# Low parts of the last expert's activations: VectorE alone instead of VectorE and GpSimd

## The chip, the cores and the metric

The kernel runs on one core of a Trainium2 chip. The metric is the device time of one execution in microseconds (us), lower is better. Engines are called as the profile calls them: PE is TensorE (PEld its weight loads), DVE is VectorE, ACT is ScalarE, POOL is GpSimd, SP is SyncE, which here only issues transfers.

## What is computed

Attention with a sliding window and four sink positions, then two mixtures of eight experts, all in float32. The first mixture gives every token to every expert and weighs the results; the second gives each token to exactly one expert, 192 tokens each, chosen greedily in the order of the gate's logits. Cut to what matters here:

```python
def _moe_ref(x, w_gate, w1, w2):          # N, D, E, F = 1536, 512, 8, 1024
    P = ...                               # gate weights, balanced over 8 rounds
    for e in range(E):
        h = np.maximum(x @ w1[e], 0.0)
        out += P[:, e:e + 1] * (h @ w2[e])

def _moe2_ref(x, w_gate, w1, w2):
    logits = x @ w_gate
    ...                                   # sort, assign each token, cap = N // E
    for e in range(E):
        mask = assigned == e
        out[mask] = np.maximum(x[mask] @ w1[e], 0.0) @ w2[e]
```

## The kernel before

A float32 product is made of three passes of a faster format: each operand is split into a high part (rounded) and a low part (what is left), and high x high, high x low and low x high are added up. For an activation tile h of 128 x 256 the high part `hh` is a copy by ACT and the low part `hl` a subtraction, h - hh.

The first mixture runs expert by expert over six groups of 256 tokens and eight chunks of 128 hidden units. Its last expert (number 7, `LE`) is done differently. Its first product (L1148, `make_pair_g1`) is finished early and its activations are kept as float32 for all groups (tiles `h7`, `xp0`, `xp1`; `h32_of`). From them `make_last_pair` makes the last expert's share of the second mixture's logits with two small matmuls for each tile (L1519, L1521), and so the logits are known before the last expert's second product is. That product is *deferred* (`make_deferred`): for each of 6 groups x 8 chunks = 48 tiles it splits h again (`make_parts`) and issues six matmuls (L1083, in `make_g2`), two for each of the three passes. So `make_parts` is called 96 times, 48 for the logits and 48 for the deferred product. Its low part is line 1553, its high part line 1550. The tiles `hh` and `hl` go round in a ring of four.

The deferred product is what PE does during the *routing* (`make_routing`), which finds for every expert the threshold of its logits. It is a chain of eight rounds. In a round DVE masks and reduces (L1675 to L1683, L1694), DVE writes eight and ACT four comparison tiles (L1688, L1691), PE counts with twelve small matmuls (L1698), DVE closes the round (L1701 to L1704), and PE broadcasts the result (L1708), for which the next L1675 waits. Then tokens are ranked, positions written (L1792), and a flag says if the simple routing holds (L1767). POOL scatters the tokens' rows into sorted order in DRAM (L1892). After the flag every engine passes a branch (L1801), whose body is not executed for these inputs. The second mixture begins with the load of the sorted rows (L1934); their memory is handed over once all deferred parts have been made. Then come the transposes (L2002, L2009) and the second mixture's products (L2043 and on).

The order of all this is not written by hand. A greedy list scheduler (`Sched`) runs when the program is built: each task has an engine or a choice of engines, a cost in us, a priority and dependences; the scheduler keeps a clock for each engine, takes the task that can start first (within a small slack the most urgent), and writes its instructions. Where a task has a choice, the engine on which it would end first gets it:

```python
k = (t + (cost if len(x.alts) > 1 else 0.0), pr)
```

Where PE's clock shows a hole ahead of its next task, `Sched.warm` writes dummy transposes of the identity (L206) into it, one for each 0.11 us of the modelled hole. These instructions stand in the program and are executed whatever the real hole is. So a change of one task's engines moves the order of everything behind it. `PLO` is the cost that the scheduler has for a low part on POOL, 0.88; on DVE it is 0.43.

Of the kernel before, what the change touches and what calls it, by code (L numbers as in the profile page):

```python
# [22 lines left out]
def tile_attention_moe_moe(ctx, tc, q, k, v, n_sink, window, wg1, w1a, w2a, wg2, w1b, w2b, out):  # L23
# [26 lines left out]
    def f32(ap):  # L50
        return ap.bitcast(F32)
# [33 lines left out]
    class Sched:  # L85
# [11 lines left out]
        def task(self, eng, cost, fn, deps=(), prio=0.0, use=(), acq=None, rel=None, name=""):  # L97
            x = Task()
            x.name = name
            x.alts = [(eng, cost)] if isinstance(eng, str) else list(zip(eng, cost))  # L100
            x.fn, x.prio, x.acq, x.rel, x.succ, x.end, x.eng = fn, prio, acq, rel, [], None, None
            d = set(deps)
            for h in use:
                assert not h.closed
                if not h.users:
                    if h.prev is not None:
                        assert h.prev.users
                        d.update(h.prev.users)
                        h.prev.closed = True
                    if h.last is not None:  # L110
                        d.add(h.last.users[0])
                h.users.append(x)
            d.discard(None)
            x.deps = list(d)
            x.left = 0
            for y in x.deps:
                if y.end is None:
                    y.succ.append(x)
                    x.left += 1
            if not x.left:  # L120
                self.ready.append(x)
            return x
# [119 lines left out]
    PLO, PSP = 0.88, 1.35  # L242
# [177 lines left out]
    task = sch.task  # L420
# [1071 lines left out]
    def h32_of(g, c):  # L1492
        if g not in H7:
            p = g // 2
            x = xp.tile([P, 2, FC, GW], F32, name=f"xp{p - 1}") if p else raws["pool"].tile([P, 2, FC, GW], F32, name="h7", bufs=1)
            H7[2 * p], H7[2 * p + 1] = x[:, 0], x[:, 1]
        return H7[g][:, c]

    def make_last_pair(k):
# [5 lines left out]
        for i in range(2):  # L1505
            g, s = 2 * p + i, ("p", k, i)
            hh_ = ring["h"].new()

            def relu(g=g, i=i):
                act(h32_of(g, fc), HS[k, 0][:, i], AF.Relu)  # L1510

            H32[g, fc] = task("ACT", 0.39, relu, deps=[prev, G1E.get(p - 1)] + [H32.get((g - i, fc))], prio=pr - 33.0 + i, use=[hph],
                              name="relu")
            a, b = make_parts(s, g, fc, hh_, pr - 29 + i)

            def gmm(i=i, s=s):
                o = bank[key][:, i * GW:(i + 1) * GW]
                hh, hl = HT[s]
                nc.tensor.matmul(o[:2 * E], W2G[:, fc].rearrange("p s e -> p (s e)"), hh, start=first and i == 0, stop=False,  # L1519
                                 skip_group_check=True)  # L1520
                nc.tensor.matmul(o[:E], W2G[:, fc, 0], hl, start=False, stop=last and i == 1, skip_group_check=True)  # L1521

            m = task("PE", 0.22, gmm, deps=[a, b, GDEP[1], LAST.get("gmm")], prio=pr - 5, use=[hh_],
                     acq=key if first and i == 0 else None, name="gmm")
            LAST["gmm"] = m
# [21 lines left out]
    def make_parts(s, g, fc, hh_, pr):  # L1547
        def hi():
            HT[s] = (wk.tile([P, GW], F32R, name="hh", bufs=4), wk.tile([P, GW], F32R, name="hl", bufs=4))
            act(HT[s][0], h32_of(g, fc), AF.Copy)  # L1550

        def lo(eng):
            (nc.gpsimd if eng == "POOL" else nc.vector).tensor_tensor(HT[s][1], h32_of(g, fc), f32(HT[s][0]), op=OP.subtract)  # L1553

        a = task("ACT", 0.41, hi, deps=[H32[g, fc]], prio=pr, use=[hh_], name="hhi")
        return a, task(("DVE", "POOL"), (0.43, PLO), lo, deps=[a], prio=pr, use=[hh_], name="hlo")

    DEF = []

    def make_deferred(q_):  # L1560

        n = n_moe1 + q_ // 2
        g = q_ // (2 * NU)
        _, _, u = uses[n]
        f = q_ % 2
        fc = 2 * u + f
        s = ("d", q_)
        k = q_ % (2 * NU)
        make_loads_for(n)
        pr = v_gem(v_use(n) + f)  # L1570
        hh_ = ring["h"].new()
        a, b = make_parts(s, g, fc, hh_, pr - 32.5)
        DEF.extend((a, b))
        make_g2(s, hh_, [a, b], pr + 5.0, (LE, g, n, f, k == 0, k == 2 * NU - 1), dyn=True)
# [676 lines left out]
```

## Time and profile before

| what | us |
|---|---|
| median of 3 runs | 1373.38 |
| lowest, highest | 1371.47, 1374.92 |
| the profiled execution's time | 1374.58 |
| its span in the profile | 1372.8 |

The profiled execution is one more execution, with its own time; the span runs from its first to its last recorded instruction. Busy times are sums over instructions of an engine. The windows view gives them for stretches of the span, with the clock that PE was granted (1.00 is 2.4 GHz, its higher level; 0.5 is 1.2 GHz, the lower one) and the mean busy share of the 16 DMA engines. The timeline view gives instructions one by one; in brackets stands the idle time just before one and what ended it. Matmuls are pipelined, so the distance from one start to the next is what one costs.

### The profile page before, as it was taken

The numbers are of one execution on the slowest core, as the hardware profiler recorded it, in microseconds if no ns is written. First come the engines' busy times: TensorE is split into PE (matmuls) and PEld (weight loads), VectorE is DVE, ScalarE is ACT, GpSimd is POOL, SyncE is SP. The second block draws the span as 40 slices with busy tenths as digits, with TensorE's granted clock in tenths as the row PEclk, the third lists the DMA queues.
The fourth block names the chain that finished last, engine by engine and source line by source line (L and its number), as shares of the span: only waits on it lengthen the run. The fifth ranks groups of instructions, "written<-read, shape, count | busy, mean of one in ns | idle before, by whom it ended". The sixth has DMA issues, their size and how long they took to land. (4 is left out here: it accounts for less than half of the span.)

```text
span 1372.8 us, 22527 instructions
## 1 busy us (share of the span) xinstructions
PE 1355.2 (99%) x8299; PEld 1173.3 (85%) x8299; DVE 928.3 (68%) x2455; ACT 620.3 (45%) x1560; POOL 112.3 (8%) x251
## 2 busy tenths in 40 slices
PE   8999999999999999999999999999999999899998
PEld 8888888988888888888998889888887777688887
DVE  8877767886455555646364645449989968568885
ACT  7777663644243333334242433331133353357874
POOL 4221110000000000000000000000001023401111
PEclk9999999999999999999999999999999999989999
DMA  7433211112020101001010101161020010458873
GB/s 172 131 78 78 63 39 47 62 47 78 0 62 16 46 17 47 31 32 47 16 62 1 63 1 62 47 202 40 16 93 16 1 47 17 131 199 263 263 225 98
DMA packets 102529, 101.47 MB, mean 74 GB/s; under 512 B 42248, under 2 KB 79112, under 8 KB 102288
## 3 DMA queue, kind: packets, MB, share of 16 engines
q1 hardware_dynamic: 100432, 93.71, 22.5%
q0 software_dynamic: 1984, 6.30, 1.5%
q8 instruction: 66, 1.08, 0.3%
q14 instruction: 47, 0.39, 0.1%
HBM read 91.71 MB, written 8.28 MB: 73 GB/s over the span
## 5 line engine op out<-in xcount | busy, mean ns | idle before, releaser
L1347 ACT ACTIVATE hh<-c 128x256 fp32r<-128x256 f32 x180 | 74.6, 415 | 124.8 <-DVE c L1314 112.2
L1148 PE MATMUL hp<-xp,w1hs 128*128 128x512 f32 x384 | 120.8, 396 | 0.0
L1314 DVE TENSOR_TENSOR c<-hp,cp 128x256 f32<-128x256 f32 x120 | 50.8, 423 | 94.7 <-PE hp L1290 89.5
L1378 PE MATMUL o<-w2ls,hh 128*128 128x512 f32 x240 | 95.0, 396 | 0.0
L1378 PE MATMUL o<-w2hs,hh 128*128 128x512 f32 x240 | 94.4, 393 | 0.0
L1378 PE MATMUL o<-w2hs,hl 128*128 128x512 f32 x240 | 94.3, 393 | 0.0
L1290 PE MATMUL hp<-xp,w1hs 128*128 128x256 f32 x480 | 88.1, 282 | 0.0
L1148 PEld LDWEIGHTS hp<-xp,w1hs 128*128 128x128 f32 x384 | 69.5, 188 | 15.1
L1350 DVE SCALAR_TENSOR_TENSOR hl<-c,hh 128x256 fp32r<-128x256 f32 x180 | 74.5, 419 | 9.4 <-ACT hh L1347 7.1
L1290 PEld LDWEIGHTS hp<-xp,w1hs 128*128 128x128 f32 x480 | 76.6, 188 | 4.7
L1553 POOL TENSOR_TENSOR hl<-h,hh 128x256 fp32r<-128x256 f32 x15 | 12.9, 857 | 789.7 <-ACT hh L1550 786.0
L1148 PE MATMUL hp<-xp,w1ls 128*128 128x512 f32 x192 | 75.8, 395 | 0.0
L1052 PE MATMUL hp<-xp,w1hs 128*128 128x256 f32 x384 | 73.9, 287 | 0.5 <-DVE xp L708 0.3
L1306 ACT ACTIVATE cu<-hp 128x256 f32<-128x256 f32 x60 | 23.1, 385 | 108.0 <-PE hp L1290 107.9
L1083 PE MATMUL o<-w2hs,hh 128*128 128x512 f32 x168 | 68.4, 407 | 1.6 <-PEq L1801 1.6
L1290 PE MATMUL hp<-xp,w1ls 128*128 128x256 f32 x240 | 67.5, 281 | 0.0
L1347 ACT ACTIVATE hh<-hp 128x256 fp32r<-128x256 f32 x60 | 23.2, 386 | 96.6 <-PE hp L1290 96.4
L882 DVE TENSOR_TENSOR w2ls<-w2r,w2hs 128x512 fp32r<-128x512 f32 x89 | 59.7, 684 | 10.4 <-DVEq L1801 6.1
L1083 PE MATMUL o<-w2ls,hh 128*128 128x512 f32 x168 | 66.5, 396 | 0.0
L1083 PE MATMUL o<-w2hs,hl 128*128 128x512 f32 x168 | 66.4, 395 | 0.0
L884 ACT ACTIVATE w2hs<-w2r 128x512 fp32r<-128x512 f32 x92 | 56.5, 624 | 18.5 <-DMA w2r<-in_moe_w_dram 11.6
L882 DVE TENSOR_TENSOR w1ls<-w1r,w1hs 128x512 fp32r<-128x512 f32 x85 | 57.9, 687 | 9.2 <-ACT w1hs L884 8.6
(484 smaller groups left out, 4028.3 us busy)
## 6 DMA issues: line engine op xcount, KB each, us to landing
w1r<-in_moe_w_dram SPq DMA_DIRECT2D x46, 512.0 KB, 4.3
w2r<-in_moe_w_dram SPq DMA_DIRECT2D x46, 512.0 KB, 3.6
wr<-in_moe_w_dram SPq DMA_DIRECT2D x46, 512.0 KB, 3.4
xs<-xs_d SPq DMA_DIRECT2D x14, 256.5 KB, 4.1
nk<-in_k_dram SPq DMA_DIRECT2D x12, 256.0 KB, 3.1
nq<-in_q_dram SPq DMA_DIRECT2D x12, 256.0 KB, 3.9
nv<-in_v_dram SPq DMA_DIRECT2D x12, 256.0 KB, 3.6
wgb<-wgd SPq DMA_DIRECT2D x1, 2048.0 KB
```

Source lines behind the costliest of these rows:

```text
L882: (nc.gpsimd if eng == "POOL" else nc.vector).tensor_tensor(lo[:, c], r[:, c], f32(hi[:, c]), op=OP.subtract)
L884: act(hi[:, c], r[:, c], AF.Copy)
L1052: nc.tensor.matmul(p, a, b, start=(c == 0 and j == 0), stop=(c == DC - 1 and j == 2), skip_group_check=True)
L1083: nc.tensor.matmul(OUTP[g, j], a_, b_, start=(first and i == 0), stop=(last and i == 2), skip_group_check=True)
L1148: nc.tensor.matmul(HS[k, 0].rearrange("p a b -> p (a b)"), a, b, start=(c == 0 and j == 0), stop=(c == DC - 1 and j == 2), skip_group_chec ...
L1290: nc.tensor.matmul(st[bk], l_[:, c], r_[:, c], start=(start and c == 0 and j == 0), stop=(c == 1 and j == 2), skip_group_check=True)
L1306: act(st[key], st[bk], AF.Copy)
L1314: tt(st[out], st[bk], st[key], op=OP.add)
L1347: act(hh, st[key], AF.Relu)
L1350: nc.vector.scalar_tensor_tensor(HT[i, f, t][1], st[key], 0.0, f32(HT[i, f, t][0]), op0=OP.max, op1=OP.subtract)
L1378: nc.tensor.matmul(OUTP[g, j % GT], a_, b_, start=(first and f == 0 and z == 0), stop=(last and f == 1 and z == 2), skip_group_check=True)
L1553: (nc.gpsimd if eng == "POOL" else nc.vector).tensor_tensor(HT[s][1], h32_of(g, fc), f32(HT[s][0]), op=OP.subtract)
```

## The change

A low part of `make_parts` could be made by DVE or POOL, whichever the scheduler's clocks showed to end it first. It is now a task of DVE alone, with the cost that DVE had.

```diff
@@ make_parts @@
         a = task("ACT", 0.41, hi, deps=[H32[g, fc]], prio=pr, use=[hh_], name="hhi")
-        return a, task(("DVE", "POOL"), (0.43, PLO), lo, deps=[a], prio=pr, use=[hh_], name="hlo")
+        return a, task("DVE", 0.43, lambda: lo("DVE"), deps=[a], prio=pr, use=[hh_], name="hlo")
```

The line also reorders the program from the last expert on. Counted over the whole order, POOL has 35 instructions of line 1553 before and none now, DVE 61 and 96, and PE has 225 dummy transposes of line 206 before and 356 now; all other counts are equal.

On POOL, around the constants of the routing (`rpiv`) and the first scatters. `h` and `xp` are the tiles that hold the activations, `acc` a group's output rows. Before:

```order
L1615 IOTA rpiv 128x128
L1553 TENSOR_TENSOR hl<-h_11287,hh 128x256 x11
L1553 TENSOR_TENSOR hl<-xp_11547,hh 128x256 x12
L1553 TENSOR_TENSOR hl<-xp_11807,hh 128x256 x3
L1891 MEMSET spacer 1x1
L1892 DMA xs_d<-acc_111,pos 3072x513
```

And now:

```order
L1615 IOTA rpiv 128x128
L1891 MEMSET spacer 1x1
L1892 DMA xs_d<-acc_111,pos 3072x513
L1891 MEMSET spacer 1x1
L1892 DMA xs_d<-acc_112,pos 3072x513
```

The 26 subtractions between the constants and the first scatter are gone from POOL (eight stood ahead of the constants, one among the scatters).

On DVE, from the comparison tiles of one routing round to the start of the next. Before:

```order
L1694 TENSOR_SCALAR rOHh<-rOHb 128x32
L1688 TENSOR_SCALAR rG<-rT,ru 128x128 x8
L1553 TENSOR_TENSOR hl<-xp_11547,hh 128x256
L1701 TENSOR_SCALAR rinc<-side_12605 8x1
L1702 SCALAR_TENSOR_TENSOR rjk,rinc<-side_12605,rinc,rdT 8x128
L1704 SCALAR_TENSOR_TENSOR rinc<-rinc 8x1
L1099 SCALAR_TENSOR_TENSOR acc_113<-side_12445,PR,acc_113 128x512
L1675 TENSOR_TENSOR rV<-rVh,o_12643 128x96
```

And now:

```order
L1694 TENSOR_SCALAR rOHh<-rOHb 128x32
L1688 TENSOR_SCALAR rG<-rT,ru 128x128 x8
L1553 TENSOR_TENSOR hl<-h_11287,hh 128x256
L1701 TENSOR_SCALAR rinc<-o_12460 8x1
L1702 SCALAR_TENSOR_TENSOR rjk,rinc<-o_12460,rinc,rdT 8x128
L1704 SCALAR_TENSOR_TENSOR rinc<-rinc 8x1
L1553 TENSOR_TENSOR hl<-h_11287,hh 128x256
L1675 TENSOR_TENSOR rV<-rVh,side_12496 128x96
```

Before, DVE had 8 low parts between the routing's first reduction (L1645) and the flag (L1767), in some rounds none; now it has 18, two in most rounds.

On PE, from one round's broadcast (L1708) on. `side`, `o` and `av` are PSUM banks, `w2hs` and `w2ls` the parts of the weights. Before, eighteen to twenty deferred matmuls stand between one broadcast and the next:

```order
L1708 MATMUL side_12296<-ident,rinc 128x8
L1083 MATMUL side_12281<-w2hs_121,hh 128x512
L1083 MATMUL av<-w2ls_122,hh 128x512
L1083 MATMUL side_12281<-w2ls_122,hh 128x512
L1083 MATMUL av<-w2hs_121,hl 128x512
L1083 MATMUL side_12281<-w2hs_121,hl 128x512
L1083 MATMUL av<-w2hs_10250,hh 128x512
L1083 MATMUL side_12281<-w2hs_10250,hh 128x512
L1083 MATMUL av<-w2ls_10251,hh 128x512
L1083 MATMUL side_12281<-w2ls_10251,hh 128x512
L1083 MATMUL av<-w2hs_10250,hl 128x512
L1083 MATMUL side_12281<-w2hs_10250,hl 128x512
```

And now, up to the round's first count:

```order
L1708 MATMUL o_12428<-ident,rinc 128x8
L1083 MATMUL av<-w2hs_10250,hl 128x512
L1083 MATMUL side_12277<-w2hs_10250,hl 128x512
L1083 MATMUL av<-w2hs_10250,hh 128x512
L1083 MATMUL side_12277<-w2hs_10250,hh 128x512
L1083 MATMUL av<-w2ls_10251,hh 128x512
L1083 MATMUL side_12277<-w2ls_10251,hh 128x512
L1083 MATMUL av<-w2hs_10250,hl 128x512
L1083 MATMUL side_12277<-w2hs_10250,hl 128x512
L206 MATMUL side_12452<-ident 128x128 x7
L1698 LDWEIGHTS rOHb
```

Between two broadcasts there are now 12 deferred matmuls and 9 dummies in the usual round, and 4 and 28 in the third and the eighth stretch. In all, 186 deferred matmuls stood between the routing's first transpose (L1649) and the flag's matmul (L1762) before, and 108 do now; from there to the branch 45 and 120, behind the branch 30 and 33.

## Rows read from the trace of the kernel before

**Rows 1.** The page's part 1, whole run: engine, busy us, share, instructions.

```profile
PE 1355.2 (99%) x8299; PEld 1173.3 (85%) x8299; DVE 928.3 (68%) x2455; ACT 620.3 (45%) x1560; POOL 112.3 (8%) x251
```

**Rows 2.** The page's part 5, costliest groups: the edited line on POOL.

```profile
L1553 POOL TENSOR_TENSOR hl<-h,hh 128x256 fp32r<-128x256 f32 x15 | 12.9, 857 | 789.7 <-ACT hh L1550 786.0
```

**Rows 3.** The edited line, whole run: who waited for it (us, times).

```profile
  PEld o L1083: 0.4, 1
```

**Rows 4.** Windows: stretch, length, busy us (instructions) by engine, PEclk, DMA share, GB/s.

```profile
1119.00:1179.20 60.20, 59.52 (x327) 43.78 (x326) 50.17 (x205) 24.28 (x68) 22.23 (x30) 1.00 0.08 27
1179.20:1189.30 10.10, 10.05 (x43) 7.73 (x42) 4.35 (x9) 4.13 (x10) 8.09 (x16) 1.00 0.87 230
...
1200.90:1211.50 10.60, 10.38 (x33) 8.98 (x34) 3.58 (x6) 1.64 (x3) 2.31 (x4) 0.52 0.46 150
```

**Rows 5.** The edited line, 1119 to 1179.2 us: count, ns min/median/max, first and last start.

```profile
L1553 POOL TENSOR_TENSOR hl<-xp,hh x15: 725/735/837, 1136.6 to 1174.4; 128x256 fp32r<-128x256 f32 x15
L1553 POOL TENSOR_TENSOR hl<-h,hh x9: 725/738/1259, 1119.6 to 1134.7; 128x256 fp32r<-128x256 f32 x9
L1553 DVE TENSOR_TENSOR hl<-xp,hh x8: 402/424/426, 1138.5 to 1179.1; 128x256 fp32r<-128x256 f32 x8
```

**Rows 6.** Timeline of DVE in the routing: start us, us, instruction, idle before.

```profile
1129.33 0.26 DVE L1675 TENSOR_TENSOR rV<-rVh,side 128x96 f32<-128x96 f32 x1 [0.51 <-PE side L1708]
...
1152.54 0.25 DVE L1675 TENSOR_TENSOR rV<-rVh,o 128x96 f32<-128x96 f32 x1 [1.20 <-PE o L1708]
...
1154.17 0.42 DVE L1694 TENSOR_SCALAR rOHh<-rOHb 128x32 bf16<-128x32 bf16 x1
...
1155.96 0.42 DVE L1553 TENSOR_TENSOR hl<-xp,hh 128x256 fp32r<-128x256 f32 x1
1156.32 0.15 DVE L1701 TENSOR_SCALAR rinc<-side 8x1 f32<-8x1 f32 x1
...
1156.88 0.15 DVE L1704 SCALAR_TENSOR_TENSOR rinc<-rinc 8x1 f32<-8x1 f32 x1
...
1158.23 0.26 DVE L1675 TENSOR_TENSOR rV<-rVh,o 128x96 f32<-128x96 f32 x1 [0.26 <-PE o L1708]
...
1166.51 0.16 DVE L1694 TENSOR_SCALAR rOHh<-rOHb 128x32 bf16<-128x32 bf16 x1
...
1169.21 0.15 DVE L1704 SCALAR_TENSOR_TENSOR rinc<-rinc 8x1 f32<-8x1 f32 x1
...
1170.31 0.26 DVE L1675 TENSOR_TENSOR rV<-rVh,o 128x96 f32<-128x96 f32 x1 [0.59 <-PE o L1708]
```

**Rows 7.** Timeline of DVE ahead of the routing.

```profile
1102.53 0.76 DVE L1553 TENSOR_TENSOR hl<-xp,hh 128x256 fp32r<-128x256 f32 x2 [2.42 <-ACT hh L1550]
```

**Rows 8.** Timeline of PE in the same round.

```profile
1152.43 0.50 PE L1083 MATMUL side<-w2ls,hh 128*128 128x512 f32 x1
1152.77 0.39 PE L1083 MATMUL o<-w2ls,hh 128*128 128x512 f32 x1
...
1155.11 0.39 PE L1083 MATMUL o<-w2hs,hh 128*128 128x512 f32 x1
...
1158.12 0.50 PE L1083 MATMUL side<-w2ls,hh 128*128 128x512 f32 x1
```

**Rows 9.** Timeline of PE at other dummies.

```profile
267.77 2.46 PE L206 MATMUL side<-ident 128*128 128x128 f32 x21
269.98 0.48 PE L1290 MATMUL hp<-tx,ehs 128*128 128x256 f32 x2
```

**Rows 10.** Timeline of POOL in the same round.

```profile
1153.78 0.78 POOL L1553 TENSOR_TENSOR hl<-xp,hh 128x256 fp32r<-128x256 f32 x1 [1.18 <-ACT hh L1550]
```

**Rows 11.** Timeline of DVE, then PE, behind the branch.

```profile
1194.51 1.29 DVE L882 TENSOR_TENSOR w2ls<-w2r,w2hs 128x512 fp32r<-128x512 f32 x2 [6.13 <-DVEq L1801]
...
1190.88 0.47 PE L1083 MATMUL o<-w2hs,hh 128*128 128x512 f32 x1 [1.64 <-PEq L1801]
...
1200.96 0.46 PE L2002 MATMUL side<-ident,xs 128*128 128x128 f32 x2 [2.63 <-DMA xs<-xs_d]
```

## The prediction

> **What bounds the kernel now.** The page's first part says that TensorE (PE) is busy 99% of the span [rows 1], so a change pays or costs only through what PE does or waits for. The costliest groups come next: 15 of the edited line's 35 runs on POOL make one of them, 857 ns each at the mean [rows 2], and over the whole run PE waited for that line once, for 0.4 us [rows 3]. So the low parts are nowhere late today. What matters is where they are made. Taken by stage [rows 4], the stretch from 1119 to 1179.2 us is the routing of the second mixture: a chain of eight rounds between DVE, ACT and PE, beside which PE works off the deferred matmuls of the last expert (L1083). PE is busy 59.5 of its 60.2 us. Every group of six L1083 needs one high part from ACT and one low part from line 1553. In this stretch 24 low parts come from POOL and 8 from DVE, 32 together [rows 5]. DVE itself is busy 50.2 of the 60.2 us there [rows 4], and its gaps stand inside the chain's own rounds, so the question is how many low parts DVE alone can fit into a round.
>
> **The change, part by part.**
>
> *Low parts leave POOL.* 35 subtractions vanish from POOL's queue. Behind them stand the scatters into the sorted rows, which may now begin as soon as their positions are known. They gain nothing by it: the first load of sorted rows is tied to the last deferred low part (its memory is handed over only then), not to the first scatter.
>
> *Low parts join DVE.* Each takes 0.36 us there from its start to that of the next instruction (1155.96 to 1156.32; 0.42 by its own row, whose end overlaps) [rows 6]. Eleven of the 35 lie outside the routing. Most of those fall beside the gating products before 1100 us; 11 x 0.36 = 4.0 us of work, and soon after it DVE stands idle for 2.42 us at one wait for ACT [rows 7]. Such gaps ahead of the routing hide them. Without them the routing would begin up to 4.0 us late.
>
> *In the routing the order changes.* The scheduler now gives DVE two low parts in a round, one before the round's close and one behind it, in the place where DVE waits for PE's broadcast; in the second round and the seventh, two accumulations stand there instead. Counted in the changed order, 18 low parts stand between the first reduction of the routing and the flag. PE so has 108 deferred matmuls from the routing's first transpose to the flag's matmul, where it had 186. The other 78 are still done, but behind the flag: 120 stand there ahead of the branch in place of 45, and 33 behind it in place of 30. One takes 0.234 us (ten steps from 1152.77 to 1155.11) [rows 8], so 78 x 0.234 = 18.3 us of PE's work moves from beside the routing to behind it.
>
> *The gaps are filled.* In the holes that its model sees, the scheduler writes 131 more dummy transposes of line 206. PE executes them whether it has a hole or not. 21 of them took from 267.77 to 269.98 us, 0.105 us each [rows 9], so 131 x 0.105 = 13.8 us.
>
> *How long a round becomes.* Now seven rounds take from 1129.33 to 1170.31 us, 5.85 us each [rows 6]. On DVE one round runs 4.34 us from its first row to the last of its close (1152.54 to 1156.88), one low part included. Its half-scaling row, L1694, took 0.42 us there and 0.16 in another round; without POOL I take the short one, 4.08 us. The turn through PE then takes 1.10 us (1169.21 to 1170.31) to 1.35 (1156.88 to 1158.23), and the second low part fits into it: 5.18 to 5.43 us. On PE the same round took 5.69 us (1152.43 to 1158.12) [rows 8] with 18 deferred matmuls, so 5.69 - 18 x 0.234 = 1.48 us go to the counts and the broadcast. With 12 deferred matmuls and 9 dummies it needs 1.48 + 2.81 + 0.94 = 5.23 us, and with 4 and 28, as in the emptiest rounds, 5.36. Both engines agree on about 5.35, which I take; 8 x 0.5 = 4.0 us shorter in all.
>
> What L1694 shows in these rows: 0.42 us while POOL's subtraction of 1153.78 ran [rows 10], 0.16 us with none beside it. The Trainium skill (SBUF — State Buffer, section "Who interferes with whom") says that VectorE, in its two-port modes or with two inputs in SBUF, needs a pair of ports that it shares with GpSimd, and that whoever comes second is blocked until the other has finished; by that rule DVE's chain gets quicker with POOL gone, and the change should gain. The rows agree with the rule, but at a few tenths of a us in a round.
>
> *The sum.* Counted by work moved: 18.3 - 4.0 = 14.3 us more. Counted by what PE executes more: 13.8 us, with its waiting about as before. I take 14.0. Behind the flag nothing else changes in length: there DVE's low part (0.36) stands against 1.41 us of matmuls that need it. The profiled execution took 1374.58 us for a span of 1372.8; it would take 1388.6. It lies 1.2 us over the median of the three runs, 1373.38, so I predict a median of **1387.4 us**.
>
> **The rivals.**
>
> *B: the tail behind the branch recovers.* The branch on the flag costs DVE 6.13 us and PE 1.64, then PE waits 2.63 us for the sorted rows, and from 1200.9 to 1211.5 us its granted clock is 0.52, the lower of its two levels, 1.2 GHz [rows 4, 11]. The branch begins while ten scatters crowd the DMA engines (a share of 0.87 from 1179.2 to 1189.3 us [rows 4]). With 120 matmuls, 28 us, between flag and branch in place of 45, some 10 us, the scatters spread out. If the branch's fetch is what they slow down, DVE comes back sooner, the rows arrive in time, and the clock stays up: 2.63 us, and half of the 10.6, some 5.0, come back, 7.6 of 14.0, at most 9.4 with PE's own stall. Time: 1379.8, at the least 1378.0. It decides once DVE's stall falls to about 3.5 us. Against it: DVE's stall ran on to 1194.51.
>
> *C: DVE becomes the bound of the round.* If the early low part delays every close by its 0.36 us and nothing is won elsewhere, rounds take 6.2 us and the routing is 2.9 us longer; even with rounds as now the 18.3 stand unreduced. Time: 1391.7 to 1394.6. For it: DVE is the busiest engine beside PE there. Against it: the same place already holds a low part or a longer accumulation in most rounds.
>
> *D: it ends on the other side, because a late low part was what held PE.* POOL needs 736 ns at the median where DVE needs 424 [rows 5]; 35 x 0.31 = 10.9 us of latency go. If PE stood behind these halves, it would gain up to that: 1362.5. It decides where PE's wait for line 1553 exceeds a few us. The one wait of 0.4 us speaks against it [rows 3], and so does the 59.5 of 60.2 us. The Trainium skill (Perfetto Trace Analysis, section "Optimizing GPSIMD Operations") advises engines other than GpSimd where possible since it is the slower one; by it the time would fall. Here the row for the operation agrees (736 against 424 ns) and the row for the wait does not.
>
> That the change does nothing is excluded by its order: 35 rows leave POOL, and 131 dummies come.
>
> **How the numbers follow.** Forecast 0.58, B 0.25, C 0.11, D 0.06 (of which 0.02 faster; 0.04 stands for a gain that just eats up the loss). A measurement of this kernel tells about 0.3%, 4.1 us, from no change. Forecast and C are slower by more than that, B too, unless all of its 9.4 us come and rounds shorten more than I think: 0.94 slower, 0.04 within, 0.02 faster. The forecast's own range is 1385 to 1390 (rounds of 5.2 to 5.5 us). The range reaches down to B's least, 1378.0, and up to the start of C, 1392.0; left out are most of C and all of D, 0.15.
>
> **What would show it.** Right: POOL without line 1553; 18 low parts on DVE within the routing; rounds of 5.2 to 5.5 us between one L1675 and the next; 131 more transposes of L206, at about 0.105 us; flag some 4 us earlier than 1179 and the branch some 14 us later than 1189; DVE again over 5 us in the branch and PE over 2 us before L2002. Wrong: PE idle between its groups within the routing for more than 0.5 us a round (C); the granted clock at 1.00 in the stretch of L2002 and L2009 (B); a flag that comes later than before.

## The result, and the profile after

The change took **1380.51 us** (median of 5 runs, 1378.87 to 1380.68) beside 1373.38 for the kernel before in the same session: ratio 1.0054, interval 1.0036 to 1.0072, so 7.1 us slower. It lies inside the forecast range and on the forecast side, and half of the 14.0 us of the likeliest sum is missing. The profiled execution took 1380.51 us for a span of 1378.7 (before 1374.58 and 1372.8): 5.9 us more.

First the page's part 1, then the windows of the routing (gate to flag), of the work between flag and branch, and of the tail behind it. Columns: stretch, length, busy us (instructions) of PE, PEld, DVE, ACT, POOL, granted clock, DMA share, GB/s.

```profile
PE 1366.1 (99%) x8430; PEld 1186.3 (86%) x8430; DVE 933.7 (68%) x2490; ACT 620.6 (45%) x1560; POOL 84.4 (6%) x216
```

```profile
1119.00:1173.40 54.40, 54.37 (x380) 43.59 (x379) 44.12 (x207) 19.00 (x55) 2.85 (x5) 1.00 0.02 7
1173.40:1201.00 27.60, 27.60 (x119) 21.97 (x117) 14.99 (x32) 8.29 (x20) 8.29 (x15) 1.00 0.45 134
1201.00:1217.80 16.80, 16.46 (x74) 13.65 (x74) 8.58 (x17) 6.21 (x12) 2.53 (x6) 0.90 0.51 168
```

PE has 131 instructions more than in [rows 1], the 131 transposes, and the share of 99% says nothing of it: a dummy counts as busy. The routing went from 60.2 us [rows 4] to 54.4. The stretch from flag to branch went from 10.1 us [rows 4] to 27.6, with PE busy in every moment of it. The last 8.4 us ahead of the new experts' products, which answer to the stretch of clock 0.52 in [rows 4], ran at 0.80:

```profile
1209.40:1217.80 8.40, 8.35 (x40) 7.50 (x41) 4.27 (x8) 2.36 (x5) 2.20 (x4) 0.80 0.52 184
```

Two more answers of the trace in the routing: line 206 and its transposes, line 1553 and its low parts.

```profile
L206 PE MATMUL side<-ident x87: 271/273/332, 1136.9 to 1168.0; 128*128 128x128 f32 x87
L206 PE MATMUL o<-ident x44: 272/273/328, 1129.8 to 1135.9; 128*128 128x128 f32 x44
```

```profile
L1553 DVE TENSOR_TENSOR hl<-h,hh x10: 404/410/418, 1119.5 to 1148.1; 128x256 fp32r<-128x256 f32 x10
L1553 DVE TENSOR_TENSOR hl<-xp,hh x8: 403/416/420, 1152.1 to 1172.2; 128x256 fp32r<-128x256 f32 x8
```

87 and 44 are the 131 transposes; 10 and 8 are the 18 low parts where there had been 32 [rows 5]. One round on DVE, then the same round on PE (start us, us, instruction, idle before it):

```profile
1149.03 0.25 DVE L1675 TENSOR_TENSOR rV<-rVh,o 128x96 f32<-128x96 f32 x1 [0.57 <-PE o L1708]
...
1150.72 0.17 DVE L1694 TENSOR_SCALAR rOHh<-rOHb 128x32 bf16<-128x32 bf16 x1
1150.84 1.40 DVE L1688 TENSOR_SCALAR rG<-rT,ru 128x128 bf16<-128x128 bf16 x8
1152.15 0.42 DVE L1553 TENSOR_TENSOR hl<-xp,hh 128x256 fp32r<-128x256 f32 x1
...
1153.20 0.15 DVE L1704 SCALAR_TENSOR_TENSOR rinc<-rinc 8x1 f32<-8x1 f32 x1
1153.28 0.41 DVE L1553 TENSOR_TENSOR hl<-xp,hh 128x256 fp32r<-128x256 f32 x1
1154.25 0.25 DVE L1675 TENSOR_TENSOR rV<-rVh,side 128x96 f32<-128x96 f32 x1 [0.57 <-PE side L1708]
```

```profile
1150.65 0.39 PE L1083 MATMUL side<-w2hs,hl 128*128 128x512 f32 x1
1150.88 0.93 PE L206 MATMUL side<-ident 128*128 128x128 f32 x7
1151.74 0.22 PE L1698 MATMUL side<-rG,rOHb 128*8 128x129 bf16 x1
...
1152.53 0.44 PE L206 MATMUL side<-ident 128*128 128x128 f32 x2
1152.72 0.72 PE L1083 MATMUL o<-w2hs,hh 128*128 128x512 f32 x2
```

Two low parts stand in the round, one ahead of the close and one in the turn through PE, and nine transposes stand on PE where matmuls did. This round took 5.22 us (1149.03 to 1154.25); from the first (1127.69) to the last (1165.15) seven took 37.46, 5.35 each. The chain's own rows on DVE are shorter without POOL beside them. L1694, before and after (ns min/median/max):

```profile
L1694 DVE TENSOR_SCALAR rOHh<-rOHb x8: 164/424/621, 1124.3 to 1166.5; 128x32 bf16<-128x32 bf16 x8
```

```profile
L1694 DVE TENSOR_SCALAR rOHh<-rOHb x8: 164/165/166, 1123.7 to 1161.4; 128x32 bf16<-128x32 bf16 x8
```

Added up over the routing, the rows from L1675 to L1704 take 36.1 us in place of 39.9, some 0.3 us less in a round: 1.9 of it is L1694, 1.2 L1679, 0.8 L1688. The Trainium skill (SBUF — State Buffer, section "Who interferes with whom") says that the two engines share a pair of ports, and by that the chain gets quicker once POOL is silent. The trace agrees, with these numbers.

Then the branch, PE and DVE. PE's matmuls start 0.234 us apart, so two take 0.47; the two at 1200.74 take 0.86 (to 1201.60), and 0.39 is all that the branch costs PE. It had cost 1.80, measured the same way: from the last matmul ahead of it in the kernel before (first line below) to the one of 1190.88 [rows 11] are 2.03 us, less the 0.234 of one step. The other two lines are the first product of the new experts, before and now.

```profile
1188.85 0.40 PE L1083 MATMUL av<-w2hs,hl 128*128 128x512 f32 x1
1212.35 0.42 PE L2043 MATMUL side<-xe,w1hs 128*128 128x384 f32 x1
1217.80 0.42 PE L2043 MATMUL side<-xe,w1hs 128*128 128x384 f32 x1
```

```profile
1200.29 0.62 PE L1083 MATMUL o<-w2hs,hh 128*128 128x512 f32 x2
1200.74 1.02 PE L1083 MATMUL o<-w2ls,hh 128*128 128x512 f32 x2
1201.60 0.63 PE L1083 MATMUL o<-w2hs,hl 128*128 128x512 f32 x2
...
1209.39 1.75 PE L2002 MATMUL av<-ident,xs 128*128 128x128 f32 x8
```

```profile
1203.18 0.43 DVE L1553 TENSOR_TENSOR hl<-xp,hh 128x256 fp32r<-128x256 f32 x1 [3.61 <-PE o L1083]
```

DVE stands 3.61 us in place of 6.13 (the bracket names PE, but the last row of L1801 on DVE stands at 1203.0, so the branch held it), and PE's wait of 2.63 us for the sorted rows [rows 11] is gone. From L2002 to the first product of the new experts (L2043) PE takes 8.4 us (1209.39 to 1217.80) in place of 11.4 (1200.96 to 1212.35), since most of it runs at the upper clock level.

The account of the two profiles, up to that first L2043 (5.45 us later than before): 131 transposes at the 0.105 us of [rows 9] are 13.8 (here one starts 0.109 us behind another at the median, and with the changes to other work around them they take 15.2); PE's idle time in the routing falls from 0.7 us to 0.0, so 13.1 remain. The branch gives back 1.4, the wait 2.6, the clock 3.0: 6.1 us net, against the 5.45 that are read there; the account is good to 1 or 2 us.

### The profile page after: what moved, and what is told of

It is laid out like the page before. It is cut to its first block, busy times and chain, and to the rows that moved or that the text cites. A ratio compares the mean times of both kernels' runs of the same rounds, so it can differ in the third digit from the quotient of the medians.

```text
span 1378.7 us, 22757 instructions
## 1 busy us (share of the span) xinstructions
PE 1366.1 (99%) x8430; PEld 1186.3 (86%) x8430; DVE 933.7 (68%) x2490; ACT 620.6 (45%) x1560; POOL 84.4 (6%) x216
## 4 chain that ended last, share of the span: by engine, by line
PE 93%; DMA 3%; DVE 2%; issue 1%; ACT 0%; POOL 0%; POOLq 0%; SPq 0%; ACTq 0%
PE hp L1290 15%; PE o L1378 12%; PE hp L1148 10%; PE o L1083 8%; PE side L1290 6%; PE side L1378 6%; PE av L1378 6%; PE hp L1052 5%; PE side L1083 2%; DMA xs_d<-acc,pos 2%; PE side L2043 2%; PE av L676 2%; PE av L1083 2%; PE o L206 1%; PE side L206 1%; PE side L656 1%
## 5 line engine op out<-in xcount | busy, mean ns | idle before, releaser
L1378 PE MATMUL o<-w2ls,hh 128*128 128x512 f32 x240 | 95.0, 396 | 0.0
L1378 PE MATMUL o<-w2hs,hh 128*128 128x512 f32 x240 | 94.4, 393 | 0.0
L1378 PE MATMUL o<-w2hs,hl 128*128 128x512 f32 x240 | 94.3, 393 | 0.0
L1148 PEld LDWEIGHTS hp<-xp,w1hs 128*128 128x128 f32 x384 | 69.5, 188 | 15.0
L1290 PEld LDWEIGHTS hp<-xp,w1hs 128*128 128x128 f32 x480 | 76.6, 188 | 4.7
L1083 PE MATMUL o<-w2hs,hh 128*128 128x512 f32 x184 | 72.3, 407 | 0.0
L1083 PE MATMUL o<-w2ls,hh 128*128 128x512 f32 x184 | 70.7, 397 | 0.1
L1083 PE MATMUL o<-w2hs,hl 128*128 128x512 f32 x184 | 70.3, 396 | 0.0
L1350 DVE SCALAR_TENSOR_TENSOR hl<-hp,hh 128x256 fp32r<-128x256 f32 x60 | 25.4, 423 | 56.9 <-ACT hh L1347 56.9
L882 DVE TENSOR_TENSOR w1ls<-w1r,w1hs 128x512 fp32r<-128x512 f32 x85 | 57.7, 685 | 8.6 <-ACT w1hs L884 8.0
L1052 PEld LDWEIGHTS hp<-xp,w1hs 128*128 128x128 f32 x384 | 60.2, 188 | 3.5 <-DVE xp L708 0.5
```

The source lines that it names most:

```text
L882: (nc.gpsimd if eng == "POOL" else nc.vector).tensor_tensor(lo[:, c], r[:, c], f32(hi[:, c]), op=OP.subtract)
L1052: nc.tensor.matmul(p, a, b, start=(c == 0 and j == 0), stop=(c == DC - 1 and j == 2), skip_group_check=True)
L1083: nc.tensor.matmul(OUTP[g, j], a_, b_, start=(first and i == 0), stop=(last and i == 2), skip_group_check=True)
L1148: nc.tensor.matmul(HS[k, 0].rearrange("p a b -> p (a b)"), a, b, start=(c == 0 and j == 0), stop=(c == DC - 1 and j == 2), skip_group_chec ...
L1290: nc.tensor.matmul(st[bk], l_[:, c], r_[:, c], start=(start and c == 0 and j == 0), stop=(c == 1 and j == 2), skip_group_check=True)
L1350: nc.vector.scalar_tensor_tensor(HT[i, f, t][1], st[key], 0.0, f32(HT[i, f, t][0]), op0=OP.max, op1=OP.subtract)
```

## The experiments

Two numbers of each profile are compared: from the routing's first reduction (L1645) to the flag, and from the flag to the first L2043. The third column is what PE stands at the branch by the start-to-start steps of its matmuls, the fourth the DMA share in the 4 us ahead of that stand, the fifth the time from the issue of the last scatter ahead of the branch to the first load of sorted rows. All come from timelines and windows.

| profile | L1645 to flag | flag to L2043 | stand | DMA share | scatter to load |
|---|---|---|---|---|---|
| before | 60.1 | 33.3 | 1.80 | 1.00 | 8.5 |
| e0_before | 60.1 | 28.6 | 3.35 | 1.04 | 7.8 |
| e1_lastpair | 60.1 | 27.6 | 2.41 | 0.91 | 6.1 |
| e4_def_first | 60.1 | 26.9 | 1.85 | 0.75 | 8.2 |
| e10_held | 60.1 | 30.0 | 4.81 | 1.02 | 10.1 |
| e9_first | 62.0 | 32.1 | 2.84 | 1.07 | 9.9 |
| e6_pool | 61.0 | 31.2 | 0.33 | 0.20 | 5.7 |
| e8_price | 58.4 | 33.7 | 0.38 | 0.28 | 5.7 |
| the change | 54.4 | 44.4 | 0.39 | 0.18 | 5.6 |
| e11_after | 54.4 | 47.0 | 0.38 | 0.19 | 5.8 |
| e2_deferred | 54.4 | 43.2 | 0.31 | 0.18 | 5.6 |
| e5_clump | 54.4 | 43.3 | 0.39 | 0.18 | 5.6 |
| e3_nofill | 54.0 | 45.3 | 0.38 | 0.18 | 5.9 |
| e5b_hold | 54.4 | 48.4 | 1.40 | 0.55 | 7.1 |

**Which low parts.** e1_lastpair: in make_parts

```
-        return a, task("DVE", 0.43, lambda: lo("DVE"), deps=[a], prio=pr, use=[hh_], name="hlo")
+        return a, task("DVE", 0.43, lambda: lo("DVE"), deps=[a], prio=pr, use=[hh_], name="hlo") if s[0] == "p" else task(("DVE", "POOL"), (0.43, PLO), lo, deps=[a], prio=pr, use=[hh_], name="hlo")
```

> Only the low parts of the last pair's logits go to the vector engine alone; the deferred ones keep their choice. The routing's order on the tensor engine is then as before: 186 deferred matmuls (L1083) beside the routing, none of the 131 transposes, 45 between flag and branch. Theory (the whole change of time comes from the deferred low parts): ratio to before 0.998 to 1.002, rounds of 5.85 us, the vector engine's wait at the branch about 6 us. Rival (vector work ahead of the routing costs up to 11 x 0.36 = 4.0 us): 1377 us, ratio about 1.003, flag at 1183 in place of 1179.05.

Measured: 1369.36 us beside 1368.79, ratio 1.0004 (0.9995 to 1.0013). The edit moves 8 of POOL's 35 low parts (its instructions go from 251 to 243). e2_deferred is the same line with "d" in place of "p".

> Only the deferred low parts go to the vector engine alone. Theory: the time of the whole change, ratio to before 1.004 to 1.007 (1379 to 1382 us), rounds of 5.35 us, 131 transposes more, the vector engine's wait at the branch 3.6 us. Rival (half of it from the last pair's low parts): ratio 1.002 to 1.003.

Measured: 1380.38 us, ratio 1.0085 (1.0072 to 1.0099). It moves the other 27. Together: the whole cost is the deferred low parts'; the eight of the last pair, all ahead of the routing, cost nothing. Of the eleven that the prediction put outside the routing the other three are deferred ones, and no run tests them alone. The ratio itself came out above the expected range: the time was that of the change (1380.5), but the kernel before ran faster beside it, 1368.8.

**How large is the cost?** e0_before and e11_after are the two kernels unchanged.

> The kernel before, unchanged, profiled once more. Theory (what the tail behind the flag costs before the change differs from one chip to another, since the kernel before took 1373.4 us beside the change and 1368.8 beside the last four runs, while the change took 1380.5 and its like 1380.4): if the time is near 1369, flag to first L2043 takes 27 to 30 us in place of the 33.3 of the first profile, with no wait of over 0.5 us for the sorted rows. Rival: the tail is always 33 us and the 4.6 us lie elsewhere.

> The change, unchanged, timed once more beside the kernel before. Theory (the change itself costs 10 to 12 us; the 7.1 us first measured were smaller because the kernel before then lost 3 to 5 us in the tail behind the flag): ratio 1.006 to 1.009, the change near 1380 whatever the chip, the kernel before between 1368 and 1374. Rival (7 us is the cost, the rest is chance): ratio 1.004 to 1.006.

Measured: e0_before 1371.28 us in its one run; beside it the same kernel had a median of 1370.59. e11_after 1380.57 beside 1371.23, ratio 1.0063 (1.0047 to 1.0079): the interval holds values of the theory and of the rival, and does not part them. The change takes 1380.4 to 1380.6 in the three sessions that timed it (e2_deferred stands for it in one), the kernel before 1368.8 to 1373.4 in four; the cost is 7 to 12 us, 9.3 here. The sessions of these runs were on three different chips. The tail of e0_before, PE and then DVE:

```profile
1193.82 0.47 PE L1083 MATMUL o<-w2hs,hh 128*128 128x512 f32 x1 [3.17 <-PEq L1801]
1202.46 1.60 PE L2002 MATMUL side<-ident,xs 128*128 128x128 f32 x8
```

```profile
1193.75 1.29 DVE L882 TENSOR_TENSOR w2ls<-w2r,w2hs 128x512 fp32r<-128x512 f32 x2 [3.23 <-DVEq L1801]
```

PE stands longer at the branch than in the first profile, and then never waits for the sorted rows; from flag to L2043 it takes 28.6 us, not 33.3. So the wait of 2.63 us and the clock of 0.52 behind it were of that execution, not of the kernel. The low clock has moved, not gone: the 30 matmuls behind the stand take 8.6 us at a granted clock of 0.80, where the first profile had 7.3 at 1.00, and the stretch of L2002 then runs at 1.00. DVE's stand is 3.23 us here and 3.00 in e1_lastpair, where about 6 was expected, so its fall to 3.61 cannot be put down to the change. The 29 executions of the kernel before beside e11_after spread from 1369.5 to 1376.4 us; the nine above 1373 have a granted clock of 0.995 to 0.997 over the whole span, the six under 1370.3 of 0.997 to 0.999. The change's tail varies as well: e11_after waits 0.90 and 0.33 us for the rows, and its tail is 2.6 us longer than that of the first profile.

**What the transposes do.** e3_nofill is the change without the dummies from L1645 to the flag: a flag set there makes the function that writes line 206 return.

```
-            if n < 1 or not (self.extra or free):
+            if rt.get("quiet") or n < 1 or not (self.extra or free):
```

> The change, with the 131 dummy transposes beside the routing left out; the deferred matmuls stand as in the change (108 beside the routing, 120 between flag and branch, 33 behind). Theory (the vector engine's chain, about 4.65 us busy with two low parts plus 0.56 us of waiting, sets the round; the transposes only fill holes): rounds of 5.2 to 5.35 us, the tensor engine idle for 10 to 13 us in the routing where it had the transposes, time within 0.2% of the change (1378 to 1382 us). Rival 1 (the transposes hold up the counts and the broadcast): rounds under 5.1 us, time 1376 to 1378 us. Rival 2 (the holes lower the granted clock of the routing below 0.95): slower than the change by over 3 us.

Measured: 1381.39 us, ratio 1.0102 (1.0085 to 1.0119); e2_deferred beside it took 1380.38. Its routing, and PE in it:

```profile
1118.90:1172.90 54.00, 46.65 (x249) 32.78 (x248) 43.86 (x207) 19.04 (x55) 2.87 (x5) 0.91 0.02 7
```

```profile
1132.24 0.35 PE L1708 MATMUL side<-ident,rinc 8*128 8x8 f32 x2 [1.15 <-DVE rinc L1704]
...
1136.90 0.63 PE L1083 MATMUL side<-w2hs,hh 128*128 128x512 f32 x1
1137.33 0.63 PE L1083 MATMUL av<-w2ls,hh 128*128 128x512 f32 x1
...
1141.07 0.39 PE L1083 MATMUL side<-w2ls,hh 128*128 128x512 f32 x1
1141.31 0.39 PE L1083 MATMUL av<-w2hs,hl 128*128 128x512 f32 x1
```

The routing is 0.5 us shorter, with rounds of 5.38 us (1127.61 to 1165.25): the transposes hold up next to nothing, they stand in holes that DVE's two low parts leave. (A lower clock, next, could hide a small gain.) PE idles 7.35 us, less than expected, since the granted clock falls to 0.91 and a matmul then starts 0.43 us behind the last (1136.90 to 1137.33) in place of 0.24 (1141.07 to 1141.31); the windows of those two moments, 1136 to 1138 and 1140 to 1142 us, have clocks of 0.50 and 0.75. So the theory holds for the time, and the second rival for the clock, though not for its 3 us. The cost of the change is work not done beside the routing; the dummies are how it shows.

**Putting the matmuls back.** Both next kernels leave every low part on DVE and change only the scheduler's book, the costs and clocks by which it orders the program, so that more of them fall into a round. e8_price:

```
-        return a, task("DVE", 0.43, lambda: lo("DVE"), deps=[a], prio=pr, use=[hh_], name="hlo")
+        return a, task("DVE", 0.05, lambda: lo("DVE"), deps=[a], prio=pr, use=[hh_], name="hlo")
```

> The change, with the low part entered in the scheduler's book at 0.05 us in place of 0.43 (the instruction is the same). The scheduler then puts up to four low parts into a round: 163 deferred matmuls beside the routing in place of 108, 43 transposes there in place of 131, 65 between flag and branch. Theory (what costs is the transposes that stand where a matmul could, 0.105 us each): 43 x 0.105 = 4.5 us over before instead of 13.8, less up to 2 for a shorter stand at the branch: ratio to before 1.002 to 1.004. Rival (the vector engine has no room for more than two low parts in a round, more of them only lengthen it): rounds of over 6 us, time as in the change or slower, ratio 1.007 to 1.012.

Measured: 1375.74 us beside 1370.59, ratio 1.0035 (1.0021 to 1.0050): as the theory has it in the sum. The profile spreads it otherwise: the routing begins at 1123.67 us, 3.3 later than in e0_before, and from there to L2043 3.4 us are lost. Of the 3.3, 1.8 are PE waiting ahead of the routing for low parts of DVE, which the book prices at 0.05 us (1.26 at one L1521, at 1092.3 us, and 0.55 at another); the rest is not explained. e9_first:

```
-        return a, task("DVE", 0.43, lambda: lo("DVE"), deps=[a], prio=pr, use=[hh_], name="hlo")
+        return a, task("DVE", 0.2, lambda: lo("DVE"), deps=[a], prio=-1001.0 if s[0] == "d" and s[1] >= AHEAD else pr, use=[hh_], name="hlo")
```

> The change, with the deferred low parts entered at 0.2 us and taken ahead of the routing's own steps. 198 deferred matmuls then stand beside the routing, no transposes, 37 between flag and branch, 26 behind. The pool engine still makes no low part. Theory (nothing is lost as long as the tensor engine always has a matmul): ratio to before 0.998 to 1.002, although the rounds lengthen to about 6.2 us; the flag comes later, at about 1182 us. Rival (a low part in the chain delays the close, and the tensor engine idles at the broadcast): idle of the tensor engine over 0.5 us a round, ratio 1.004 or more.

Measured: 1373.99 us, ratio 1.0019 (1.0009 to 1.0030). Routing, then tail:

```profile
1119.50:1181.50 62.00, 61.77 (x338) 45.69 (x338) 54.20 (x231) 24.93 (x70) 3.19 (x5) 1.00 0.08 26
1181.50:1213.60 32.10, 26.83 (x109) 21.30 (x107) 12.29 (x24) 8.36 (x17) 9.90 (x21) 0.84 0.72 178
```

DVE alone can feed PE after all: rounds of 6.03 us, PE idle for 0.23 us in the whole routing, so the rival falls. What is still lost lies in the tail, which has the crowded branch again (stand 2.84, then two waits of 1.09 and 0.89 us for the rows, clock 0.84). e6_pool is the mirror, with the deferred low parts on POOL alone:

```
+        return a, task("POOL", 0.78, lambda: lo("POOL"), deps=[a], prio=pr, use=[hh_], name="hlo") if s[0] == "d" else task(("DVE", "POOL"), (0.43, PLO), lo, deps=[a], prio=pr, use=[hh_], name="hlo")
```

> The mirror of the change: the deferred low parts are made by the pool engine alone, entered at 0.78 us. 184 deferred matmuls then stand beside the routing and no transpose, but eight low parts stand behind eight scatters in the pool engine's queue, and 49 transposes between flag and branch fill the hole. Theory (dummies cost what they take, wherever they stand): 49 x 0.105 = 5.1 us, less what the rounds gain (0.1 to 0.2 us each without low parts on the vector engine): ratio to before 1.002 to 1.005. Rival (the vector engine's free time shortens the routing by over 3 us and pays for them): ratio under 1.001.

Measured: 1373.97 us beside 1371.23, ratio 1.0017 (1.0007 to 1.0026), at the low end of the theory. Its transposes, from the timeline of PE:

```profile
1180.56 5.51 PE L206 MATMUL o<-ident 128*128 128x128 f32 x49
```

5.51 us are paid there, and the routing is 0.9 us longer (61.0), so the rival falls; beside the first two rows of the table 1.5 to 3.0 come back at the branch, which holds PE up for 0.33 us, with a DMA share of 0.20 ahead of it. So who makes the low part matters little in itself. Ordered by dummies added: none +2.6 us by the ratio (e9_first, 0.0019 of 1370.6), 43 +4.8, 49 +2.3, 131 +7 to +12; 43 and 49 stand the other way round, so the count alone does not set the cost.

**What the branch waits for.** e5_clump holds the scatters in the scheduler's book until the eighth row tile is accumulated.

```
-            SCT.append(task("POOL", 1.1, lambda t=t: scatter(t), deps=[place_, CB[t]] + ZR, prio=t, name="scatter"))
+            SCT.append(task("POOL", 1.1, lambda t=t: scatter(t), deps=[place_, CB[t], CB[7]] + ZR, prio=t, name="scatter"))
```

> The change, with all ten scatters held until the eighth row tile is accumulated (about 1187 us), so that they are issued back to back in the 13 us ahead of the branch, as before the change; no other engine's order moves (120 deferred matmuls between flag and branch, 33 behind it). Theory (the transfers in flight at the branch set how long the engines stand there): the vector engine's wait at the branch goes from 3.6 back to 5.5 to 6.5 us, the tensor engine's from 0.2 to about 1.6, then the tensor engine waits 1.5 to 3 us for the sorted rows and its granted clock falls behind it: 1384 to 1388 us, that is the sum the prediction took. Rival (the wait at the branch depends on what the engines do around it, not on the scatters): waits as in the change, time within 0.2% of 1380.5.

Measured: 1381.44 us, ratio 1.0098 (1.0082 to 1.0113). The edit failed: the book orders a queue and adds no wait on the chip, POOL issued its first scatter at 1169.96 us as in the change, and the run is one more copy of it. e5b_hold puts the eighth tile's scatter first in POOL's queue, so that its data hold the rest.

```
-        for t in range(NE):
+        for t in [7, 0, 1, 2, 3, 4, 5, 6, 8, 9]:
-            SCT.append(task("POOL", 1.1, lambda t=t: scatter(t), deps=[place_, CB[t]] + ZR, prio=t, name="scatter"))
+            SCT.append(task("POOL", 1.1, lambda t=t: scatter(t), deps=[place_, CB[t]] + ZR + SCT, prio=t, name="scatter"))
```

> The change, with the scatter of the eighth row tile written first, so that its data (accumulated at about 1187 us) hold all ten on the in-order queue; they are issued back to back from 1188 to 1201 us, just ahead of the branch. Nothing moves on another engine (120 deferred matmuls between flag and branch, 33 behind). Theory (transfers in flight at the branch set how long the engines stand there): share of the DMA engines over 0.6 from 1192 to 1202 us, the tensor engine stands 1.5 us or more at the branch in place of 0.2 to 0.4, the vector engine 5 us or more in place of 3.6, time 2 to 6 us over the change. Rival (what else they do decides, not the transfers): as in the change, within 0.15%, except for a later load of sorted rows.

Measured: 1381.89 us beside 1370.59, ratio 1.0077 (1.0063 to 1.0092). POOL's first scatter, PE behind the branch and at the sorted rows, DVE, and the 4 us ahead of the stand; then the same 4 us in the change:

```profile
1187.59 1.17 POOL L1892 DMA_INDIRECT xs_d<-acc,pos  x1 [86.98 <-DVE acc L1099]
```

```profile
1202.05 0.47 PE L1083 MATMUL o<-w2ls,hh 128*128 128x512 f32 x1 [1.22 <-issue]
...
1211.54 1.78 PE L2002 MATMUL av<-ident,xs 128*128 128x128 f32 x8 [1.53 <-DMA xs<-xs_d]
```

```profile
1204.48 0.42 DVE L1553 TENSOR_TENSOR hl<-xp,hh 128x256 fp32r<-128x256 f32 x1 [5.18 <-PE o L1083]
```

```profile
1196.40:1200.40 4.00, 4.00 (x18) 3.21 (x18) 2.22 (x5) 1.25 (x3) 3.33 (x7) 1.00 0.55 204
```

```profile
1196.70:1200.70 4.00, 4.00 (x18) 3.22 (x18) 2.20 (x5) 1.25 (x3) 2.00 (x3) 1.00 0.18 70
```

Nothing moved on PE and DVE, and each wait came back, if not to its full size: PE 1.40 at the branch (0.31 to 0.39 in four profiles of the change), DVE 5.18, the load of the rows 7.1 us behind the last scatter in place of 5.6, then 1.53 us of waiting. In the profile the first L2043 is 1.2 to 5.2 us later than in those four. In the timed runs the effect is not resolved: 1381.9 against 1380.4 to 1381.4. The table says the same of fourteen profiles: with a DMA share of 0.28 or less the stand is 0.3 to 0.4 us, with 0.75 or more it is 1.8 to 4.8. The stand is only what is left of the branch once PE has run out of matmuls queued ahead of it. The branch itself is the row of L1801 on PE's weight-load sequencer, which reaches it some 3 us earlier: the change, e5b_hold, before, e0_before (ns; start):

```profile
L1801 PEldq COMPARE_BRANCH  x1: 3322/3322/3322, 1197.4 to 1197.4; - x1
L1801 PEldq COMPARE_BRANCH  x1: 4602/4602/4602, 1197.3 to 1197.3; - x1
L1801 PEldq COMPARE_BRANCH  x1: 5222/5222/5222, 1185.5 to 1185.5; - x1
L1801 PEldq COMPARE_BRANCH  x1: 6542/6542/6542, 1187.1 to 1187.1; - x1
```

Over the fourteen profiles it lasts 3.3 to 3.8 us with a share of 0.28 or less, and 5.0 to 8.0 (e10_held) with 0.75 or more. That instructions come over the same engines is in the DMA view of the change, from 1185 to 1205 us (packets, MB, share):

```profile
q8 instruction: 2, 0.03, 0.9%
```

One such packet, of 16 KB, lies inside the branch's row in each of the fourteen profiles, and the row ends 1.3 to 2.3 us after it has landed. It lands 1.8 us behind the row's start in the change, 2.5 in e5b_hold, 3.1 in the first profile of before, 5.3 in e0_before and 5.6 in e10_held. That it is this branch's own fetch is inferred from its place.

The Trainium skill (Runtime: NRT & Kernel Launch, section "Instruction fetch mechanics") says that a taken branch to a place not yet fetched waits for a DMA of the target's page; it gives no time for it. The rows agree and give the times above.

**Can the tail be mended in the kernel before?** e4_def_first makes the branch's task depend on all deferred low parts; e10_held has that edit and also means to hold one more weight load (the second pair of lines).

```
-        return task("X", 0.0, general, deps=SCT + [flag], name="general")
+        return task("X", 0.0, general, deps=SCT + [flag] + DEF, name="general")
-... + (SCT[NE - 1:NE] if 1 <= need - n_defer < 3 else []), prio=pr - 21, ...
+... + (SCT[NE - 1:NE] if 0 <= need - n_defer < 3 else []), prio=pr - 21, ...
```

> The kernel before, with the branch held until all deferred low parts are made: 57 deferred matmuls between flag and branch in place of 45, 18 behind it in place of 30; no transpose more. Theory (the transfers in flight at the branch set how long the engines stand, and they thin out by the 2.8 us that the branch comes later): the tensor engine stands under 1.5 us at the branch in place of 2.2, but waits for the sorted rows 1 to 3 us, since 18 matmuls cover 4.2 us in place of 7.0: time within 0.2% of before. Rival (the wait for the rows hangs on the low parts behind the branch): they arrive 2 to 3 us earlier and the time falls by 2 us or more.

> The kernel before, with the branch held until all deferred low parts are made and the weight load of 512 KB that is issued at 1180 us held back until the last scatter ahead of the branch is issued. Theory (transfers at the branch): the scatters land earlier, the tensor engine stands under 1 us at the branch, the sorted rows come 1 to 3 us earlier than in the kernel with the branch held alone; time 0 to 3 us under before, ratio 0.998 to 1.000. Rival (the load is then late for the split of the next weights): a wait for w2r of over 1 us behind the branch and a ratio over 1.001.

Measured: e4_def_first 1371.13 us beside 1371.23, ratio 0.9997 (0.9985 to 1.0010); e10_held 1372.70, ratio 1.0010 (0.9997 to 1.0023). In e4_def_first the time is as its theory has it, but the stand is not: 1.85 us, where under 1.5 was expected. e4_def_first on SP and POOL, e10_held on PE and SP:

```profile
1197.52 0.95 SPq L1934 DMA_DIRECT2D xs<-xs_d  x2
```

```profile
1197.60 0.29 POOL L1967 IOTA slot<- 128x192 f32 x1 [7.32 <-DMA xs_d<-acc,pos]
```

```profile
1196.41 0.47 PE L1083 MATMUL o<-w2hs,hh 128*128 128x512 f32 x1 [4.65 <-PEq L1801]
```

```profile
1180.01 0.38 SPq L865 DMA_DIRECT2D w2r<-in_moe_w_dram  x1
```

With no low part left behind the branch, the rows are still loaded only at 1197.52, together with POOL's step that waits for the scatters to land: the load hangs on the last scatter's landing, and the rival (on the low parts) falls. In e10_held the load was not held, which still went out at 1180.01, by the same mistake as e5_clump; its stand of 4.8 us, the longest, came at a share of 1.02. No version beats the kernel before.

## Why the prediction was right and where it was wrong

- **What held, and by what.** 1380.5 lies inside the stated range only in the part that rival B gave it; the forecast's own range, 1385 to 1390, missed by 4.5 us. The session helped: its kernel before, at 1373.4 us, was the slowest of the four.
- **Right: the direction and its cause.** 78 deferred matmuls moved behind the flag (194 of L1083 stand in the window of the routing before, 116 after), 131 transposes took their place, at about the price forecast (0.109 us between two of them, 0.105 forecast). e1_lastpair and e2_deferred put all of it on the deferred low parts; e8_price and e9_first, with fewer dummies, lose less.
- **Right: the low parts ahead of the routing are free**, as far as tested: eight of the eleven (e1_lastpair, 1.0004). Right too are the rounds: 5.35 us.
- **Mis-sized: "8 x 0.5 = 4.0 us shorter in all".** The rounds came as forecast, but the routing fell by 5.7 us: the seven rounds gave 3.5 (41.0 to 37.5), the stretch from L1645 to the first L1675 1.7 (10.39 to 8.73; in it the eight L1688 took 2.44 us beside POOL and 1.40 without), the end 0.5. By work moved the sum is then 18.3 - 5.7 = 12.6, by work executed 13.1. The branch came 11.9 us later on PE (1188.85 to 1200.74), where some 14 were forecast.
- **Wrong, the step that failed: "Behind the flag nothing else changes in length".** The sum took the branch, the wait for the rows and the clock as before. With 120 matmuls between flag and branch in place of 45, the transfers have thinned out when the branch comes (a share of 0.18 ahead of it in place of 1.00). In the two profiles compared that gave back 1.4, 2.6 and 3.0 us. This is rival B, in its mechanism, its place and almost its size (forecast 7.6). e5b_hold shows the mechanism for the stands and the landing of the scatters. B's own sign, DVE's stand at about 3.5 us, came (3.61) but tells nothing, since e0_before and e1_lastpair have it with the old tail. B's "at most 9.4" is 7.6 with a stand of 1.80; with the row it names, 1.64, it is 9.2.
- **What of B is not of the change:** only the stand of PE (1.8 to 3.4 us down to 0.4) came back each time. The wait of 2.63 us is in the first profile of the kernel before and absent in two others with the same tail (28.6 and 27.6 us), where the low clock stands behind the branch and costs less (1.3 us in e0_before); so 14.0 was too high by some 2 to 7 us, according to the session. Why an execution of one kernel has the wait and the next has not stays open, and so does whether the chip has a part in it.
- **Wrong in a detail:** that the first load of sorted rows is tied to the last deferred low part. It issued within 0.1 us of the step that waits for the scatters' landing in e0_before, e1_lastpair, e4_def_first and the change; in the first profile of before it came 1.1 us behind it. There SP had a weight load to issue first (L865, 1195.83 us), which waited for the split on DVE (L882) that the stand of 6.13 us had delayed; so 1.1 of the 2.63 us of PE's wait came by way of DVE.
- **Rival C** (DVE bounds, longer rounds) did not come: 5.35 us. **Rival D** (a late low part held PE) falls: no run that takes low parts off POOL gains. The Trainium skill (Perfetto Trace Analysis, section "Optimizing GPSIMD Operations") advises other engines than GpSimd where possible, since it is generally the slower. For the one operation the rows agree (424 ns against 735 to 738 [rows 5]); for the kernel they do not, which lost 7 to 12 us, since POOL's slower parts ran beside DVE's chain.

## What to carry to other kernels

Where a scheduler fills holes with dummy work, a busy share of 99% hides a loss: count the dummies that a change adds, and read each as a matmul that will have to be done later. Moving work off a slow engine costs its throughput, even where each piece gets faster; ask what the faster engine was already the clock of. Before pricing the tail behind a branch or a gather "as before", look at what is on the DMA engines when it comes, and look at more than one profile of the same kernel.

## What was not expected of the hardware

What a branch held PE up went from 0.3 us to 4.8 with the load of the DMA engines (the branch's own row from 3.3 to 8.0), and the time from the last scatter's issue to the load of its rows from 5.6 us to 10.1. Leaving out the transposes, which compute nothing, lowered the granted clock of the routing from 1.00 to 0.91: some matmuls there ran at the lower of the two levels (1.2 GHz), after PE had idled at the broadcast. A dependency that exists only in a scheduler's book moved no instruction in time, twice.
